# Moving a chunked attention's later units by a few pieces inside a stream of dense matmuls

## The chip, the cores and the metric

The kernel runs on one core of a Trainium2 chip. The metric is the device time of one execution in microseconds (us), the median over the runs shown. The engines are named as the profile names them: PE (TensorE matmul), PEld (its weight loads), DVE (VectorE), ACT (ScalarE), POOL (GpSimd) and SP (SyncE, whose queue issues nearly all transfers, "SPq").

## The reference

Two parts stand one behind the other. First a causal linear attention with decay, for 4 batches, 8 heads, 768 positions and a head width of 64:

```
state = gamma[None, :, None, None] * state + np.einsum('bhd,bhe->bhde', k[:, :, t], v[:, :, t])
y[:, :, t] = scale * np.einsum('bhd,bhde->bhe', q[:, :, t], state)
```

Then y is laid out as 3072 tokens of 512 features and goes through a feed-forward block with 2048 hidden features:

```
h = x @ w_in
g = np.maximum(h, 0.0) + np.log1p(np.exp(-np.abs(h)))
return g @ w_out
```

Everything is float32 in and out. The weights arrive as 64-bit floats and are converted in the kernel.

## The kernel before, in words

**Attention units.** The attention is cut into 48 units: 4 batches, 6 chunks of 128 positions each, and 2 halves of 4 heads; unit n has chunk c = (n // 2) % 6. Units 0 to 11 (n below WHOLE) are computed in plain float32. Units 12 to 47, the "later units", split each operand into a high and a low part so that TensorE can take them in its faster one-pass form. A later unit goes through these parts:

- `load_unit`/`load_ahead`: 8 small transfers each for k and q in blocks (tiles kb and qb, or kbys and qbys from a ring of three; line 151), and one each for k and v by tokens (line 178), all issued from SP's queue.
- `decay`: POOL multiplies q (line 205) and v (206) by decay factors.
- `operands`: DVE transposes the blocks (234), ACT and DVE write the high and low parts into kq (238, 239, 241, 242, 243) and vhl (246, 247).
- `scores_first`, `scores_second`: two pairs of matmuls into a PSUM tile sc (273), each summed by a DVE reduction (274); after the second POOL masks (251), ACT rounds to ah (287) and POOL makes the rest al (288).
- `new_state`: matmuls into stp (303).
- `stack_and_outputs`: 20 small matmuls into the PSUM tile yp (351; 12 for the first chunk of a batch), two ACT copies out of it (374), the split into xh (ACT, 375) and xl (DVE, 376); then the state's split (323, 325).

For the later units sc and yp share a single PSUM bank (`attention_bank`, tag "a", one buffer). So the first scores of unit n+1 cannot start until both copies of line 374 have emptied unit n's yp, and the second scores not until the reduction of line 274 has read the first.

**The feed-forward steps.** Four units make a pair of 256 tokens. In a step s, `hidden(s)` multiplies by w_in (lines 423 to 425, three matmuls make one "piece"), `softplus` works on the result (DVE 431, ACT 432, DVE 436, ACT 438 to gh, POOL 440 to gl), and `second(s-2)` multiplies the step before the last by w_out (456 to 458, again three matmuls to a piece). From step 12 on ("paced" steps) a step is 4 hidden pieces and then 4 second pieces, slots 0 to 7. gh has two buffers, so the gh of a step is written once the second pieces of the same step have read the older one.

**What sets the order.** A counter of ticks says when each part of each unit is issued: `PARTS` gives the tick of each part relative to 16 n, since a unit comes every 16 ticks. In the paced steps one tick falls to one piece, and the PE order there is the written one; a turn of 8 steps covers 64 ticks. The other engines, and PE before step 12, are ordered by the scheduler of the tile framework, which may put an instruction ahead of its place in the program. `ticks_for(p)` says up to which tick the work must be issued before the turn of pair p+1 begins; this fixes to which slot a tick falls. Before, outputs (tick 20) fall behind the first second piece of a step, slot 4, and the next unit's first scores (tick 7 of the next 16) behind slot 7, three pieces later.

**Weights.** `convert_weights(f)` turns the 64-bit numbers of one of 16 slices into high and low parts (85 to 98) on ACT, DVE and POOL; `convert_to(n)` issues conversions up to slice n. In steps 4 to 11 a step uses two slices.

Of the kernel before, what the change touches and what calls it, by code (L numbers as in the profile page):

```python
# [19 lines left out]
TWO = 2 * C  # L20
PLACES = 3
WIDE = 512
AHEAD = 2
EARLY = 2
WHOLE = 12
THIRD = 19
TURN = 4
# [6 lines left out]
def decay_attention_then_softplus_ffn(ctx: ExitStack, tc: tile.TileContext, q, k, v, w_in, w_out, qtab, vtab, gtab, out):  # L34
# [74 lines left out]
    def place_of(p):  # L109
        return p if p < PLACES else (1, 0, 2)[p % PLACES]  # L110
# [100 lines left out]
    def attention_bank(n, shape, name):  # L211
        taken.append(n)
        if n < WHOLE and len(taken) % 2:
            return ps_o.tile(shape, F32, name=name, tag="acc3")
        return ps_a.tile(shape, F32, name=name, tag="a")
# [34 lines left out]
    def mask(a):  # L250
        nc.gpsimd.affine_select(a, a, pattern=[[0, HH], [1, C]], compare_op=ALU.is_ge, fill=0.0, base=0, channel_multiplier=-1)  # L251

    def scores_whole(n):
        if n >= WHOLE:
            return
        kq = live[n][0]
        a = attn.tile([P, HH, C], F32, name="a")
        sc = attention_bank(n, [P, HH, C], "sc")
        for h in range(HH):
            nc.tensor.matmul(sc[:, h, :], lhsT=kz[:, h % 2, h // 2, :], rhs=kq[:, h // 2, :], start=True, stop=True)  # L260
        nc.scalar.copy(a, sc)
        mask(a)
        live[n].append(a)
# [3 lines left out]
    def scores_of_pair(n, j):  # L267
        kq = live[n][0]
        if j == 0:
            summed[n] = attn.tile([P, HH, C], F32, name="a")  # L270
        sc = attention_bank(n, [P, 2, 2, C], "sc")
        for par in range(2):
            nc.tensor.matmul(sc[:, par], lhsT=kq[:, 0, par, j, :], rhs=kq[:, 1:, par, j, :], start=True, stop=True)  # L273
        nc.vector.tensor_reduce(summed[n][:, 2 * j:2 * j + 2, :], sc.rearrange("p h t c -> p h c t"), axis=mybir.AxisListType.X, op=ALU.add)  # L274

    def scores_first(n):
        if n >= WHOLE:
            scores_of_pair(n, 0)

    def scores_second(n):  # L280
        if n < WHOLE:
            return
        scores_of_pair(n, 1)
        a = summed.pop(n)
        mask(a)
        ah, al = (attn.tile([P, HH, C], F32R, name=nm) for nm in ("ah", "al"))
        nc.scalar.copy(ah, a)  # L287
        nc.gpsimd.tensor_tensor(al, a, ah.bitcast(F32), op=ALU.subtract)  # L288
        live[n] += [ah, al]
# [90 lines left out]
        stack_state(n)  # L380


    PARTS = {-24: load_unit, -40: load_ahead, -8: decay, 0: operands, 7: scores_first, 8: scores_whole, 10: scores_second, 12: new_state, 20: stack_and_outputs}
    FIRST_TICK = -24
    PERIOD = 16
    TICK = 4
    last_tick = PERIOD * (len(units) - 1) + max(PARTS)

    def tick(n):
        for at, part in PARTS.items():  # L390
            u, r = divmod(n - at, PERIOD)
            if r == 0 and 0 <= u < len(units):
                part(u)
# [12 lines left out]
    def begins(s, p):  # L406
        return s == 0 or p not in steps[s - 1][0]
# [4 lines left out]
    acc, part, hps, sps, gs = {}, {}, {}, {}, {}  # L412
# [31 lines left out]
    def second(s):  # L444
        pairs, fs = steps[s]
        gh, gl = gs.pop(s)
        places = sorted(place_of(p) for p in pairs)
        for p in pairs:
            if begins(s, p):
                odd = p % 2 or p == 0  # L450
                acc[p] = [ps_o.tile([P, DM], F32, name=f"acc{t}", tag=f"acc{t}") for t in ((0, 1) if odd else (2, 3))]
        for k, p, t in ((k, p, t) for k in range(len(fs)) for p in pairs for t in range(2)):
            at = places.index(place_of(p)) * TWO + t * P
            first, last = begins(s, p) and k == 0, ends(s, p) and k == len(fs) - 1
            wt, ts, to = wout[fs[k]], slice(at, at + P), acc[p][t]
            nc.tensor.matmul(to, lhsT=gh[:, k, ts], rhs=wt[:, 0], start=first, stop=False)  # L456
            nc.tensor.matmul(to, lhsT=gh[:, k, ts], rhs=wt[:, 1], start=False, stop=False)  # L457
            nc.tensor.matmul(to, lhsT=gl[:, k, ts], rhs=wt[:, 0], start=False, stop=last)  # L458
            if last:
                write_out(p, t, s < TURN)  # L460
            yield
# [13 lines left out]
        nc.sync.dma_start(out[row:row + P, :], o)  # L475

    def ticks_for(p):
        return min(PERIOD * 4 * (p + 1) + max(PARTS) - PERIOD + TICK + TICK * AHEAD, last_tick + TICK)

    done, loaded, converted = FIRST_TICK, 0, 0  # L480

    def convert_to(n):
        nonlocal loaded, converted
        while converted < min(NF, n):
            convert_weights(converted)
            converted += 1
            if loaded < NF:
                load_weights(loaded)
                loaded += 1
# [105 lines left out]
    for s, (pairs, fs) in enumerate(steps[:ordered]):  # L595
        if s == TURN:
            block_decays()
        convert_to(fs[-1] + 1)
        stages(s)
        convert_to(2 * max(fs[-1] // 2 + 1, s + 1 if s < TURN else TURN + (s - TURN) // 2) + EARLY)  # L600

    with tc.manual_schedule(engines={mybir.EngineType.PE}):
        for s in range(ordered, len(steps) + LAG):
# [31 lines left out]
```

## Time and profile before

| what | value |
|---|---|
| time, median of 3 runs | 701.84 us (701.45 to 701.94) |
| the profiled execution's own time | 701.68 us |
| its span | 700.0 us |
| PE busy | 662.1 us (95%) |
| DVE, ACT, POOL busy | 60%, 52%, 44% of the span |
| granted PE clock, mean over the span | 0.988 |

The time of the profiled execution is 1.68 us more than its span: the span counts from the first instruction recorded to the last. A row of the timeline gives the start in us from the span's start, the duration, the engine, line, operation and tiles, and in brackets the idle time of that engine just before it and what ended it. A row of the waits gives the total idle time, the number of waits and the longest. A row of the windows gives, for a stretch, the busy time of PE, PEld, DVE, ACT and POOL, then the granted clock, the share of the transfers' engines and GB/s.

### The profile page before, as it was taken

What the parts mean: (1) busy time and instruction counts of PE and PEld (TensorE: products, weight loads), DVE (VectorE), ACT (ScalarE), POOL (GpSimd) and SP (SyncE); (2) the same over time, 40 slices, a digit from 0 to 9 for tenths busy, and PEclk for the clock granted to TensorE, in tenths of its full rate; (3) what the DMA queues carried; (4) which work ended last, traced back from release to release, by engine and by line L of the source; (5) the groups of instructions that cost most, each with busy time, mean ns of one, the idle gap of its engine ahead of it and who ended that gap; (6) DMA issues with size and microseconds to landing.
All of it is one profiled execution on the core that took longest, in us unless ns stands there. A gap on an engine that the chain in (4) does not pass through costs nothing.

```text
span 700.0 us, 11837 instructions
## 1 busy us (share of the span) xinstructions
PE 662.1 (95%) x3762; PEld 556.8 (80%) x3762; DVE 417.4 (60%) x756; ACT 361.1 (52%) x799; POOL 310.1 (44%) x330
## 2 busy tenths in 40 slices
PE   7899998789899989999999989999999999999997
PEld 6789997668778777888888778878878888888896
DVE  4778898655568566565756656566567655432221
ACT  5888875534546455555545545465465545422221
POOL 4887766433344533453443434444534533232221
PEclk9999999899999999999999999999999999999999
DMA  9897662121132231132131223122212200000000
GB/s 243 229 281 204 174 171 49 30 67 33 30 75 47 47 76 29 22 78 39 35 79 34 36 41 72 20 39 70 44 33 67 40 8 30 1 1 31 0 31 30
DMA packets 153822, 46.69 MB, mean 67 GB/s; under 512 B 140448, under 2 KB 148640, under 8 KB 153760
## 3 DMA queue, kind: packets, MB, share of 16 engines
q1 hardware_dynamic: 153312, 45.93, 27.6%
q8 instruction: 29, 0.48, 0.3%
q14 instruction: 33, 0.27, 0.1%
q10 hardware_dynamic: 448, 0.01, 0.0%
HBM read 39.60 MB, written 6.29 MB: 66 GB/s over the span
## 4 chain that ended last, share of the span: by engine, by line
PE 52%; ACT 12%; SPq 8%; DVE 8%; DMA 7%; issue 4%; ACTq 0%; POOL 0%; DVEq 0%; POOLq 0%
PE hp L423 9%; PE hp L425 9%; PE hp L424 9%; SPq L151 7%; PE acc L456 7%; PE acc L457 7%; PE acc L458 7%; ACT kq L242 3%; DVE sp L431 3%; ACT kq L241 3%; PE sc L273 3%; DMA kb<-in_k_dram 2%; DMA qb<-in_q_dram 2%; PE stp L303 2%; PE yp L351 2%
## 5 line engine op out<-in xcount | busy, mean ns | idle before, releaser
L440 POOL TENSOR_TENSOR gl<-sp,gh 128x512 fp32r<-128x512 f32 x96 | 124.0, 1292 | 265.4 <-ACT gh L438 263.1
L423 PE MATMUL hp<-xh,winhl 128*128 128x512 f32 (+1 forms) x448 | 163.0, 364 | 1.3 <-ACT winhl L97 0.8
L424 PE MATMUL hp<-xl,winhl 128*128 128x512 f32 (+1 forms) x448 | 162.9, 364 | 0.0
L425 PE MATMUL hp<-xh,winhl 128*128 128x512 f32 (+1 forms) x448 | 162.0, 362 | 0.2 <-POOL winhl L98 0.2
L456 PE MATMUL acc<-wouthl,gh 128*128 128x512 f32 x384 | 156.1, 407 | 2.0 <-ACT gh L438 2.0
L457 PE MATMUL acc<-wouthl,gh 128*128 128x512 f32 x384 | 151.3, 394 | 0.0
L458 PE MATMUL acc<-wouthl,gl 128*128 128x512 f32 x384 | 150.6, 394 | 0.0
L432 ACT ACTIVATE sp<-sp 128x512 f32<-128x512 f32 x96 | 60.4, 630 | 138.6 <-DVE sp L431 138.5
L431 DVE TENSOR_SCALAR sp<-hp 128x512 uint32<-128x512 uint32 x96 | 65.7, 685 | 105.1 <-PE hp L425 103.2
L425 PEld LDWEIGHTS hp<-xh,winhl 128*128 128x128 f32 x448 | 85.2, 190 | 14.1 <-POOL winhl L98 0.6
L423 PEld LDWEIGHTS hp<-xh,winhl 128*128 128x128 f32 x448 | 85.1, 190 | 12.6 <-ACT winhl L97 1.0
L424 PEld LDWEIGHTS hp<-xl,winhl 128*128 128x128 f32 x448 | 85.2, 190 | 10.5
L438 ACT CAST gh<-sp 128x512 fp32r<-128x512 f32 x96 | 59.5, 619 | 57.7 <-PE acc L457 30.0
L456 PEld LDWEIGHTS acc<-wouthl,gh 128*128 128x128 f32 x384 | 73.0, 190 | 15.3 <-ACT gh L438 2.4
L458 PEld LDWEIGHTS acc<-wouthl,gl 128*128 128x128 f32 x384 | 72.3, 189 | 15.6
L457 PEld LDWEIGHTS acc<-wouthl,gh 128*128 128x128 f32 x384 | 73.1, 190 | 12.8
L436 DVE SCALAR_TENSOR_TENSOR sp<-hp,sp 128x512 f32<-128x512 f32 x96 | 64.9, 677 | 26.4 <-ACT sp L432 25.6
L251 POOL TENSOR_SCALAR_AFFINE_SELECT a<-a 128x512 f32<-128x512 f32 x48 | 35.8, 747 | 53.3 <-DVE a L274 47.6
L274 DVE TENSOR_REDUCE a<-sc 128x256 f32<-128x512 f32 x72 | 49.4, 687 | 15.3 <-PE sc L273 14.3
L273 PEld LDWEIGHTS sc<-kq 128*128 128x128 f32 x144 | 25.2, 191 | 34.6 <-ACT kbys L374 11.4
L288 POOL TENSOR_TENSOR al<-a,ah 128x512 fp32r<-128x512 f32 x36 | 47.7, 1325 | 11.3 <-ACT ah L287 9.6
L273 PE MATMUL sc<-kq 128*128 128x256 f32 x144 | 32.3, 307 | 18.5 <-ACT kbys L374 7.0
(94 smaller groups left out, 908.3 us busy)
## 6 DMA issues: line engine op xcount, KB each, us to landing
win<-in_moe_w_in_dram SPq DMA_DIRECT2D x16, 512.0 KB, 4.8
wout<-in_moe_w_out_dram SPq DMA_DIRECT2D x16, 512.0 KB, 4.6
vn<-in_v_dram SPq DMA_DIRECT2D x48, 128.0 KB, 2.8
out_dram<-o SPq DMA_DIRECT2D x24, 256.0 KB, 2.2
vn<-in_k_dram SPq DMA_DIRECT2D x30, 128.0 KB, 2.3
kb<-in_k_dram SPq DMA_DIRECT2D x208, 16.0 KB, 1.7
qb<-in_q_dram SPq DMA_DIRECT2D x208, 16.0 KB, 1.7
qn<-in_q_dram SPq DMA_DIRECT2D x12, 128.0 KB, 4.7
```

What stands on the lines that cost most here:

```text
L273: nc.tensor.matmul(sc[:, par], lhsT=kq[:, 0, par, j, :], rhs=kq[:, 1:, par, j, :], start=True, stop=True)
L423: nc.tensor.matmul(to, lhsT=wt[:, 0, d, :], rhs=xh[:, d], start=d == 0, stop=False)
L424: nc.tensor.matmul(to, lhsT=wt[:, 0, d, :], rhs=xl[:, d], start=False, stop=False)
L425: nc.tensor.matmul(to, lhsT=wt[:, 1, d, :], rhs=xh[:, d], start=False, stop=d == ND - 1)
L431: nc.vector.tensor_scalar(sp.bitcast(U32), hps[s].bitcast(U32), 0x80000000, None, op0=ALU.bitwise_or)
L432: nc.scalar.activation(sp, sp, AF.Softplus)
L436: nc.vector.scalar_tensor_tensor(g, hps.pop(s), 0.0, g, op0=ALU.max, op1=ALU.add)
L438: nc.scalar.copy(gh, g)
L440: nc.gpsimd.tensor_tensor(gl, sps.pop(s), gh.bitcast(F32), op=ALU.subtract)
L456: nc.tensor.matmul(to, lhsT=gh[:, k, ts], rhs=wt[:, 0], start=first, stop=False)
L457: nc.tensor.matmul(to, lhsT=gh[:, k, ts], rhs=wt[:, 1], start=False, stop=False)
L458: nc.tensor.matmul(to, lhsT=gl[:, k, ts], rhs=wt[:, 0], start=False, stop=last)
```

## The change

Four things are edited:

1. For the later units (`of_others`) the parts move: loads from tick -24 to -20, the two scores from 7 and 10 to 14 and 17, the state from 12 to 18, outputs from 20 to 26. Operands stay at 0 and decay at -8. The table for units 0 to 11 (`of_whole`) is as before.
2. `ticks_for` gives 16 ticks beyond 64 (p + 1) for pairs 0 and 1, as before, and 19 for later pairs (16 before). So outputs now fall behind slot 7, the end of a step, the first scores behind slot 3, four hidden pieces later, and the second scores behind slot 6.
3. In the one step in which both pairs of a turn begin, `second` takes the pairs in reversed order.
4. `convert_to` at the end of steps 4 to 8 asks for slices 12, 13, 14, 15 and 16, where it asked for 10, 10, 12, 12 and 14.

```
-AHEAD = 2
+AHEAD = 9
...
-    PARTS = {-24: load_unit, -40: load_ahead, -8: decay, 0: operands, 7: scores_first, 8: scores_whole, 10: scores_second, 12: new_state, 20: stack_and_outputs}
+
+    def of_whole(part):
+        return lambda n: part(n) if n < WHOLE else None
+
+    def of_others(part):
+        return lambda n: part(n) if n >= WHOLE else None
+
+    PARTS = {-24: of_whole(load_unit), -20: of_others(load_unit), -40: load_ahead, -8: decay, 0: operands}
+    PARTS.update({8: of_whole(scores_whole), 12: of_whole(new_state), 20: of_whole(stack_and_outputs)})
+    PARTS.update({14: of_others(scores_first), 17: of_others(scores_second), 18: of_others(new_state), 26: of_others(stack_and_outputs)})
...
+        if len(pairs) > 1 and all(begins(s, p) for p in pairs):
+            pairs = pairs[::-1]
...
-        return min(PERIOD * 4 * (p + 1) + max(PARTS) - PERIOD + TICK + TICK * AHEAD, last_tick + TICK)
+        return min(PERIOD * 4 * (p + 1) + (PERIOD if p < 2 else max(PARTS) - PERIOD + AHEAD), last_tick + TICK)
...
-        convert_to(2 * max(fs[-1] // 2 + 1, s + 1 if s < TURN else TURN + (s - TURN) // 2) + EARLY)
+        convert_to((2 * (s + 1) if s < TURN else TURN + s + 2) + EARLY)
```

The rows of the changed kernel below carry its own line numbers (423 to 425 are 427 to 429 there, 456 to 458 are 462 to 464, 351 is 346, 273 is 271, 303 is 298, 432 is 436, 438 is 442, 440 is 444, 374 is 369, 375 is 370, 323 is 318, 287 is 282, 288 is 283; lines up to 251 keep theirs).

**PE, a later unit in the paced steps.** Before, from the outputs (yp) to the next unit's first scores (sc):

```order
L351 MATMUL yp<-al,vhl 64x128 x4
L456 MATMUL acc_4697<-wouthl,gh 128x512
...
L456 MATMUL acc_5270<-wouthl,gh 128x512
...
L456 MATMUL acc_5271<-wouthl,gh 128x512
L457 MATMUL acc_5271<-wouthl,gh 128x512
L458 MATMUL acc_5271<-wouthl,gl 128x512
L273 MATMUL sc<-kq_84 128x256 x2
L423 MATMUL hp<-xh,winhl 128x512
```

and now:

```order
L464 MATMUL acc_5271<-wouthl,gl 128x512
L346 MATMUL yp<-kq_84,st_5172 64x128 x2
...
L346 MATMUL yp<-al,vhl 64x128 x4
L427 MATMUL hp<-xh,winhl 128x512
L428 MATMUL hp<-xl,winhl 128x512
L429 MATMUL hp<-xh,winhl 128x512
...
L271 MATMUL sc<-kq_85 128x256 x2
L462 MATMUL acc_4696<-wouthl,gh 128x512
```

Three second pieces stood between; now it is the four hidden pieces of the next step, with the scores in front of its second pieces.

**ACT at the same place.** sp and gh are the softplus, 241, 242 and 238 the operands of the unit after next, st the state, the copies qbys<-yp empty the bank. Before:

```order
L432 ACTIVATE sp<-sp 128x512
L241 CAST kq_85<-qb 64x256
L242 CAST kq_85<-qb 64x256
L241 CAST kq_85<-qb 64x256
L323 CAST st_4426<-stp 64x128 x2
L242 CAST kq_85<-qb 64x256
L374 COPY qbys<-yp 64x256 x2
L246 CAST vhl<-vn_90 128x4x64
L438 CAST gh<-sp 128x512
L375 CAST xh<-qbys 128x2x128
```

and now:

```order
L442 CAST gh<-sp 128x512
L241 CAST kq_85<-qb 64x256
L242 CAST kq_85<-qb 64x256
L241 CAST kq_85<-qb 64x256
L318 CAST st_4453<-stp 64x128 x2
L242 CAST kq_85<-qb 64x256
L369 COPY qbys<-yp 64x256 x2
L246 CAST vhl<-vn_90 128x4x64
L370 CAST xh<-qbys 128x2x128
L436 ACTIVATE sp<-sp 128x512
```

The run of operand writes, state and copies is the same; gh moved from behind the copies to ahead of the operand writes, and the next step's softplus stands behind all of it.

**PE where the paced steps begin (about 115 us).** hp of 128x256 is step 11, the last before the paced steps, hp of 128x512 is step 12; the last half of step 11 needs the slice of w_in that is converted last. Before:

```order
L303 MATMUL stp<-vn_90 128x128 x2
L423 MATMUL hp<-xh,winhl 128x512
...
L273 MATMUL sc<-kq_84 128x256 x2
...
L423 MATMUL hp<-xh,winhl 128x256
...
L456 MATMUL acc_1038<-wouthl,gh 128x512
...
L425 MATMUL hp<-xh,winhl 128x256
...
L273 MATMUL sc<-kq_84 128x256 x2
L351 MATMUL yp<-ah,vhl 64x128 x8
```

and now:

```order
L429 MATMUL hp<-xh,winhl 128x512
L271 MATMUL sc<-kq_84 128x256 x2
L427 MATMUL hp<-xh,winhl 128x256
L428 MATMUL hp<-xl,winhl 128x256
L429 MATMUL hp<-xh,winhl 128x256
...
L271 MATMUL sc<-kq_84 128x256 x2
L298 MATMUL stp<-vn_90 128x128 x2
L427 MATMUL hp<-xh,winhl 128x512
...
L346 MATMUL yp<-ah,vhl 64x128 x8
```

One piece of step 12 stands ahead of the last half of step 11, where four stood; the other three, and four second pieces of step 10, now stand between the second scores and yp. On ACT, DVE and POOL everything up to here is in the order of before, the weight conversions among it, except that ACT writes the very last slice of w_out ahead of the state st.

**POOL in the paced steps.** gl belongs to the softplus, qb to the decay of a unit further on, a to the mask. Before:

```order
L440 TENSOR_TENSOR gl<-sp,gh 128x512
L251 AFFINE_SELECT a<-a 128x512
L205 TENSOR_TENSOR qbys<-qbys,qblocks 128x256
L288 TENSOR_TENSOR al<-a,ah 128x512
L440 TENSOR_TENSOR gl<-sp,gh 128x512
```

and now:

```order
L444 TENSOR_TENSOR gl<-sp,gh 128x512
L205 TENSOR_TENSOR qb<-qb,qblocks 128x256
L251 AFFINE_SELECT a<-a 128x512
L444 TENSOR_TENSOR gl<-sp,gh 128x512
L283 TENSOR_TENSOR al<-a,ah 128x512
```

The decay of q moved ahead of the mask, and one gl ahead of al.

More of the change, by code (lines that the diff above doesn't have):

```diff
@@ L253, in scores_whole @@
     def scores_whole(n):
-        if n >= WHOLE:
-            return
         kq = live[n][0]
@@ L276, in scores_first @@
     def scores_first(n):
-        if n >= WHOLE:
-            scores_of_pair(n, 0)
+        scores_of_pair(n, 0)
     def scores_second(n):
-        if n < WHOLE:
-            return
         scores_of_pair(n, 1)
```

## Prediction

> **What bounds the kernel now.** I read the busy table first, then PE's waits, the windows for the granted clock, and the timeline of single units.
>
> ```profile
> PE 662.1 (95%) x3762; PEld 556.8 (80%) x3762; DVE 417.4 (60%) x756; ACT 361.1 (52%) x799; POOL 310.1 (44%) x330
> ```
>
> PE is the bound: nothing is gained by making another engine faster, only by taking PE's idle and slow time away. The work of PE itself does not change. Its waits after the first 100 us, those that matter here:
>
> ```profile
> PE sc L273 <- ACT kbys L374: 7.0, 10, 1.9
> PE sc L273 <- ACT qbys L374: 5.9, 11, 1.1
> PE yp L351 <- ACT ah L287: 4.6, 1, 4.6
> PE sc L273 <- ACT vn L374: 4.1, 4, 2.5
> PE acc L456 <- ACT gh L438: 2.0, 1, 2.0
> PE sc L273 <- DVE a L274: 1.4, 2, 0.8
> PE hp L423 <- ACT winhl L97: 0.8, 1, 0.8
> ```
>
> 25 of them, 17.0 us in all, are one thing: the first scores of a later unit wait for the copies (374) that empty the bank of the previous unit's yp. And PE runs at half clock for a while after the longer ones:
>
> ```profile
> 125.00:150.00 25.00, 21.59 (x100) 17.37 (x100) 15.38 (x26) 11.04 (x26) 10.28 (x10) 0.83 0.23 52
> 175.00:200.00 25.00, 21.70 (x110) 17.66 (x109) 15.90 (x29) 12.55 (x31) 8.56 (x10) 0.93 0.18 34
> 400.00:450.00 50.00, 47.09 (x251) 38.63 (x252) 29.89 (x55) 25.00 (x58) 21.37 (x23) 0.97 0.22 46
> ...
> 142.29 0.47 PE L456 MATMUL acc<-wouthl,gh 128*128 128x512 f32 x1 [1.97 <-ACT gh L438]
> ...
> 144.45 0.63 PE L457 MATMUL acc<-wouthl,gh 128*128 128x512 f32 x1
> ```
>
> Clocks of 0.83, 0.93 and 0.97 are (0.17 x 25) + (0.07 x 25) + (0.03 x 50) = 7.5 us lost; about 0.8 of it falls into idle time, so 6.7 us count, behind four waits (4.6, 2.0 and the longest two for line 374), 1.7 each. The last two rows show it: behind an idle 1.97 us a matmul of 512 columns lasts 0.63 us instead of the usual 0.4.
>
> **The main edit: outputs at a step's end, scores four pieces later.** A usual unit before, PE first and then ACT:
>
> ```profile
> 507.12 0.28 PE L351 MATMUL yp<-kq,st 128*64 128x128 f32 x2
> ...
> 508.32 0.45 PE L456 MATMUL acc<-wouthl,gh 128*128 128x512 f32 x1
> ...
> 511.02 0.50 PE L273 MATMUL sc<-kq 128*128 128x256 f32 x2 [0.40 <-ACT qbys L374]
> ...
> 510.22 0.74 ACT L374 COPY qbys<-yp 64x256 f32<-64x256 f32 x2
> ```
>
> ACT empties the bank at 510.96, 3.84 us after yp began, because the operand writes and the state stand ahead of the copies in its order. PE has 1.20 us of yp and three pieces to do meanwhile. One unit near the end of the attention already stands as the change puts all of them, since the last turn's ticks slide against the pieces (PE, ACT, DVE):
>
> ```profile
> 592.35 0.28 PE L351 MATMUL yp<-kq,st 128*64 128x128 f32 x2
> ...
> 593.54 0.45 PE L423 MATMUL hp<-xh,winhl 128*128 128x512 f32 x1
> ...
> 596.36 0.40 PE L273 MATMUL sc<-kq 128*128 128x256 f32 x2
> ...
> 598.69 0.50 PE L273 MATMUL sc<-kq 128*128 128x256 f32 x2
> ...
> 595.35 0.74 ACT L374 COPY qbys<-yp 64x256 f32<-64x256 f32 x2
> ...
> 596.90 0.42 DVE L376 TENSOR_TENSOR xl<-qbys,xh 128x256 fp32r<-128x256 f32 x1
> ```
>
> There four hidden pieces take 596.36 - 593.54 = 2.82 us, 0.705 each, the bank is empty at 596.09, 3.74 us after yp began, and the scores follow at 4.01 us without a wait. The slack is 0.27 us, and nothing in the changed ACT order stands ahead of the copies that did not stand there in this unit. So the 25 waits go. Each costs more than its idle time: by three pieces of 0.705 from 508.32 the scores were due at 510.44 and came at 511.02, 0.58 us later, of which 0.40 idle; the other 0.18 is refilling PE. Saved: 17.0 + 25 x 0.18 = **21.5 us**. The two DVE waits (1.4 + 0.4) go too, **1.8**; one of them returns as a rival below.
>
> What takes their place: the second scores need the reduction (274) of the first, three pieces after them. In unit 592.35 they start at 598.69, where 596.36 + 0.23 + 3 x 0.69 = 598.66 was due, and their own row is 0.50 instead of 0.40 long: 0.13 us in all. I charge this for all 33 later units that have a successor in such a place: **4.3 us**. The bounds are 0 and the 0.65 + 0.18 of the unit in the next fence, 27.4; the value is taken near the low end, from the row in the same order.
>
> Loads at tick -20 instead of -24 come four pieces, 2.8 us, later in the program. All 16 block transfers and the two by tokens of a unit move with them, in SP's queue. I cost it at nothing, because those transfers wait for a free buffer and not for their place:
>
> ```profile
> SPq L151 <- DVE kq L243: 79.3, 27, 4.4
> SPq L151 <- DVE kq L239: 50.6, 32, 6.2
> ...
> 395.67 0.28 PE L351 MATMUL yp<-kq,st 128*64 128x128 f32 x2
> ...
> 395.58 0.45 DVE L234 STREAM_TRANSPOSE kb<-kb 128x256 f32<-128x256 f32 x1 [3.44 <-DMA kb<-in_k_dram]
> ...
> 398.52 3.83 SPq L151 DMA_DIRECT2D qb<-in_q_dram  x8
> ...
> qb<-in_q_dram SPq DMA_DIRECT2D x208, 16.0 KB, 1.7
> ```
>
> The 395.58 row is a late transfer that holds DVE; before, the transpose stood ahead of the step's softplus (431), which delayed sp, the operand writes and the copies, hence the longer waits of the list. In the changed order it stands behind the softplus, so up to about 2 us of lateness ends in DVE's idle time. If that cover goes, the third rival below has the price.
>
> **Where the paced steps begin.** Here yp of the first later unit waited 4.6 us for ah right behind its scores. Now three hidden and four second pieces (7 x 0.69 = 4.8 us) and stp stand between, and saved are 4.6 + 0.18 = **4.8 us**. The wait of 2.0 for gh at 142.29 was the last link of the same congestion (+0.18: **2.2**). The half clock behind all these waits is the **6.7** worked out above. But one stall is new:
>
> ```profile
> 115.59 0.48 PE L423 MATMUL hp<-xh,winhl 128*128 128x512 f32 x1
> ...
> 116.92 0.62 ACT L97 CAST winhl<-w 128x512 fp32r<-128x512 f32 x1 [2.75 <-DVE w L95]
> ...
> 117.62 1.30 POOL L98 TENSOR_TENSOR winhl<-w,winhl 128x512 fp32r<-128x512 f32 x1 [1.19 <-ACT winhl L97]
> ...
> 126.13 1.11 PE L351 MATMUL yp<-ah,vhl 128*64 128x128 f32 x8 [4.63 <-ACT ah L287]
> ```
>
> The last half of step 11 needs the high part of its weights (117.54) and then the low part (118.92). Before, step 12 filled PE until then. Now one piece (0.7) and the scores (0.25) fill it from about 115.23, without stp, to 116.2: PE idles 1.3 us, runs two matmuls, and idles 1.1 us more. With 2 x 0.18 of refill that is 2.8, and 2.4 us idle within 3 us should halve the clock as 1.97 did; the clock's share of one such wait is 1.7. Charged: **4.5 us**; bounds 0 (the weights come earlier) and, should the half clock last twice as long, 6.2.
>
> [...]
>
> **Weights a step sooner: nothing.** Up to the high part of the last w_in slice the four engines keep the order of before; the scheduler had already put conversions where their inputs allow. So the 0.8 us wait for winhl stays, and I count no gain. The reversed pairs of one step start on the accumulators that are not just being emptied:
>
> ```profile
> 141.47 0.68 DVE L473 COPY o<-acc 128x512 f32<-128x512 f32 x1
> ```
>
> This copy ends at 142.15, as gh does, so the reversal helps to take away the 2.2 already counted and brings nothing of its own.
>
> **The sum.** 21.5 + 1.8 + 4.8 + 2.2 + 6.7 = 37.0 removed, 4.3 + 4.5 = 8.8 added: 28.2 less. The profiled span of 700.0 becomes 671.8, and with the 1.68 us between span and time **673.5 us** (the profiled execution, 701.68, stands 0.16 below the median).
>
> **The rivals.**
>
> *The second scores become the new wait.* The unit before the one above, PE, DVE and POOL:
>
> ```profile
> 584.03 0.51 PE L273 MATMUL sc<-kq 128*128 128x256 f32 x2 [0.65 <-DVE a L274]
> ...
> 581.95 1.31 DVE L376 TENSOR_TENSOR xl<-kbys,xh 128x256 fp32r<-128x256 f32 x1 [0.40 <-ACT xh L375]
> ...
> 581.69 1.29 POOL L440 TENSOR_TENSOR gl<-sp,gh 128x512 fp32r<-128x512 f32 x1 [6.42 <-ACT gh L438]
> ```
>
> Here xl on DVE stretched from 0.42 to 1.31 us beside gl on POOL; the reduction behind it came late, and PE idled 0.65. If that happens in every unit, 33 x 0.83 = 27.4 replaces 4.3: 673.5 + 23.1 = 696.6. Against it: gh, and so gl, now starts as yp does and is over 2 us later, when xl, at about 4.5 us, is still to come. For it: other POOL work could fall there. [...]
>
> *The transfers of the two-buffer units stay late.* In units 13 to 19 the loads have only two buffers. If three of them still stall as before at 178 us (2.5 idle, 0.2 refill, 1.5 of half clock: 4.2 each), it is 673.5 + 12.6 = 686. For it: SP's queue waits 130 us for DVE; against it: the two us of cover above.
>
> *The weights do come sooner.* Then the new stall of 4.5 and the old 0.8 + 0.18 vanish: 668. Against it is the unchanged order.
>
> The rows of POOL for the last rival:
>
> ```profile
> L205 POOL TENSOR_TENSOR qb<-qb,qblocks 128x256 f32<-128x256 f32 x26 | 16.5, 636 | 9.2 <-DMA qb<-in_q_dram 7.0 <-DMA kb<-in_k_dram 1.6 <-DMA vn<-in_v_dram 0.4
> L251 POOL TENSOR_SCALAR_AFFINE_SELECT a<-a 128x512 f32<-128x512 f32 x48 | 35.8, 747 | 53.3 <-DVE a L274 47.6
> L288 POOL TENSOR_TENSOR al<-a,ah 128x512 fp32r<-128x512 f32 x36 | 47.7, 1325 | 11.3 <-ACT ah L287 9.6
> ```
>
> *Slower: POOL's decay holds the mask.* qb (205) now stands ahead of the mask (251). In the unit of 395.67 its eight transfers are issued by 402.35 and the last lands 1.7 later, 8.4 us after yp began. POOL's qb (0.64), mask (0.75), gl (1.29) and al (1.33) follow, so al is ready near 12.4 us; the next yp begins after about 13 (16 pieces of 0.69, yp, the scores, stp) and needs al 1.0 later: 1.6 us of slack. It decides once qb lands more than 1.6 us later. Should the four-tick delay come through in full, 2.8 us, each unit loses 1.2 + 0.18, and 33 of them 46: 673.5 + 46 = 719. Against it: the transfers are bound by buffers, not by ticks.
>
> **How the numbers follow.** Forecast (673.5, its own range 667 to 680): 0.65. Late transfers (686): 0.13. Second scores (697): 0.11. Weights sooner (668): 0.06. Slower (719): 0.05. The range 666 to 692 leaves out the slower case, the upper part of the second scores, and a little below: under 0.2. All cases but the last are faster by more than 0.2%, 1.4 us, which is about what a measurement of this kernel can tell from no change; some of the second-scores case might end there, so faster 0.92, same 0.03, slower 0.05.
>
> **What would show it.** Right: the waits of sc for line 374 all but gone; PE's idle total from 150 to 600 us down to a few us; a granted clock of 1.00 in the windows from 150 us on; one stall of about 2.4 us near 117 us for winhl, and yp of the first later unit without a wait. Wrong: sc waiting for the reduction in most units with xl stretched (second scores), DVE held by kb or qb with PE idle behind it (transfers), or yp waiting for al (slower).

## The result, and the profile after

The changed kernel takes 673.77 us (672.65 to 674.67 in 4 runs), beside 701.64 us (700.34 to 701.94) of the kernel before on the same chip: a ratio of 0.9605, with a 95% interval of 0.9586 to 0.9624. The forecast was 673.5. The profiled execution took 673.9 us, with a span of 672.1.

The busy times of the changed kernel, from the head of its page, and PE's waits behind the start (total idle us, number, longest):

```profile
PE 654.8 (97%) x3762; PEld 553.8 (82%) x3762; DVE 414.9 (62%) x756; ACT 367.8 (55%) x799; POOL 311.6 (46%) x330
...
PE sc L271 <- DVE a L272: 3.2, 3, 1.2
PE hp L427 <- ACT winhl L97: 1.5, 2, 0.8
PE hp L429 <- POOL winhl L98: 1.0, 2, 0.8
PE sc L271 <- ACT kbys L369: 0.7, 2, 0.4
PE sc L271 <- ACT vn L369: 0.3, 1, 0.3
PE sc L271 <- DVE xl L338: 0.3, 1, 0.3
```

The first scores waited 17.0 us for ACT's copies; now it is 1.0. The 4.6 us of the first later unit's outputs and the 2.0 us for gh are gone from the list. The stall for converted weights is new, and the second scores' waits for the reduction (272) grew from 1.4 to 3.2 us.

The windows of the changed kernel (length, busy us of PE, PEld, DVE, ACT, POOL, then the granted clock, share of the transfers' engines, GB/s):

```profile
100.00:125.00 25.00, 22.18 (x120) 18.78 (x119) 21.72 (x38) 14.41 (x31) 15.62 (x16) 0.93 0.27 51
125.00:150.00 25.00, 25.00 (x136) 21.02 (x135) 18.49 (x31) 13.99 (x31) 14.00 (x14) 1.00 0.28 63
175.00:200.00 25.00, 25.00 (x143) 20.59 (x142) 16.10 (x32) 13.40 (x31) 11.95 (x13) 1.00 0.31 66
400.00:450.00 50.00, 49.70 (x281) 41.38 (x281) 31.35 (x58) 28.13 (x64) 23.91 (x24) 1.00 0.24 48
```

Where the clock was 0.83, 0.93 and 0.97, it is 1.00. One slow stretch is left, from 117.4 to 120.8 us, at these two rows of the timeline; the second already runs at half clock:

```profile
116.42 0.39 PE L427 MATMUL hp<-xh,winhl 128*128 128x256 f32 x1 [0.74 <-ACT winhl L97]
...
117.77 0.58 PE L429 MATMUL hp<-xh,winhl 128*128 128x256 f32 x1 [0.85 <-POOL winhl L98]
```

A steady unit, from its outputs to the next unit's (PE, then ACT's copies in a unit of the same kind):

```profile
312.74 0.28 PE L346 MATMUL yp<-kq,st 128*64 128x128 f32 x2
...
316.76 0.40 PE L271 MATMUL sc<-kq 128*128 128x256 f32 x2
319.09 0.50 PE L271 MATMUL sc<-kq 128*128 128x256 f32 x2
326.04 0.28 PE L346 MATMUL yp<-kq,st 128*64 128x128 f32 x2
...
383.11 0.74 ACT L369 COPY qbys<-yp 64x256 f32<-64x256 f32 x2
```

The copies end 383.85 - 380.10 = 3.75 us after that unit's yp (380.10), and the scores come 4.02 us after theirs, without a wait. The unit takes 13.30 us. The three waits for the reduction (at 159, 214 and 373 us, 0.8 to 1.2 us each) come from late transfers. The last of them, DVE first and then PE:

```profile
369.16 0.45 DVE L234 STREAM_TRANSPOSE kb<-kb 128x256 f32<-128x256 f32 x1 [3.69 <-DMA kb<-in_k_dram]
...
371.81 0.69 DVE L435 TENSOR_SCALAR sp<-hp 128x512 uint32<-128x512 uint32 x1
372.42 0.68 DVE L272 TENSOR_REDUCE a<-sc 128x256 f32<-128x512 f32 x1
...
373.15 0.50 PE L271 MATMUL sc<-kq 128*128 128x256 f32 x2 [0.78 <-DVE a L272]
```

A late kb held DVE 3.69 us, everything behind it slid without a gap, and the reduction came after the second scores were due.

### The profile page after: what moved, and what is told of

Read it like the earlier page. It is cut to its first block, busy times and chain, and to the rows that moved or that the text cites. A ratio compares the mean times of both kernels' runs of the same rounds, so it can differ in the third digit from the quotient of the medians.

```text
span 672.1 us, 11849 instructions
## 1 busy us (share of the span) xinstructions
PE 654.8 (97%) x3762; PEld 553.8 (82%) x3762; DVE 414.9 (62%) x756; ACT 367.8 (55%) x799; POOL 311.6 (46%) x330
## 4 chain that ended last, share of the span: by engine, by line
PE 73%; DVE 9%; ACT 6%; DMA 5%; SPq 3%; issue 2%; POOL 1%; DVEq 0%; POOLq 0%; ACTq 0%
PE acc L462 10%; PE acc L463 10%; PE acc L464 10%; PE hp L427 10%; PE hp L429 10%; PE hp L428 10%; PE yp L346 5%; SPq L151 3%; PE sc L271 3%; DMA kb<-in_k_dram 3%; PE stp L298 2%; DVE kq L239 2%; DVE sp L435 1%; PE sc L258 1%; DVE kq L243 1%
## 5 line engine op out<-in xcount | busy, mean ns | idle before, releaser
L444 POOL TENSOR_TENSOR gl<-sp,gh 128x512 fp32r<-128x512 f32 x96 | 128.1, 1335 | 130.0 <-ACT gh L442 125.7
L427 PE MATMUL hp<-xh,winhl 128*128 128x512 f32 (+1 forms) x448 | 166.6, 372 | 2.1 <-ACT winhl L97 1.5
L429 PE MATMUL hp<-xh,winhl 128*128 128x512 f32 (+1 forms) x448 | 162.6, 363 | 1.0 <-POOL winhl L98 1.0
L462 PE MATMUL acc<-wouthl,gh 128*128 128x512 f32 x384 | 150.9, 393 | 0.0
L463 PE MATMUL acc<-wouthl,gh 128*128 128x512 f32 x384 | 150.2, 391 | 0.0
L464 PE MATMUL acc<-wouthl,gl 128*128 128x512 f32 x384 | 149.0, 390 | 0.0
L462 PEld LDWEIGHTS acc<-wouthl,gh 128*128 128x128 f32 x384 | 72.2, 188 | 12.3
L463 PEld LDWEIGHTS acc<-wouthl,gh 128*128 128x128 f32 x384 | 72.3, 188 | 12.0
L205 POOL TENSOR_TENSOR qb<-qb,qblocks 128x256 f32<-128x256 f32 x26 | 17.2, 663 | 87.1 <-ACT gh L442 27.0
L206 POOL TENSOR_TENSOR vn<-vn,vtabs 128x256 f32<-128x256 f32 x48 | 30.7, 639 | 38.5 <-DMA vn<-in_v_dram 25.7
L251 POOL TENSOR_SCALAR_AFFINE_SELECT a<-a 128x512 f32<-128x512 f32 x48 | 33.5, 699 | 21.2 <-DVE a L272 14.5
```

The lines of the kernel that those rows point to most:

```text
L427: nc.tensor.matmul(to, lhsT=wt[:, 0, d, :], rhs=xh[:, d], start=d == 0, stop=False)
L429: nc.tensor.matmul(to, lhsT=wt[:, 1, d, :], rhs=xh[:, d], start=False, stop=d == ND - 1)
L444: nc.gpsimd.tensor_tensor(gl, sps.pop(s), gh.bitcast(F32), op=ALU.subtract)
```

## The experiments

Diffs marked "after" are against the changed kernel, those marked "before" against the kernel before. Times are medians of four runs (two where both are given), and each ratio is to runs of the kernel before on the same chip. The runs were made on several chips, so two of them are also compared by their ratios, where a difference of 0.001 stands for 0.7 us.

### Is it the distance or the place?

The prediction took the outputs' new place and the added piece as one edit. Three kernels part them, though none has the new place alone at three pieces: the first of them keeps the reversed pairs, the later loads and the earlier conversion of the change.

*One piece less, place as changed (after):*

```
-PARTS.update({14: of_others(scores_first), 17: of_others(scores_second), ...
+PARTS.update({13: of_others(scores_first), 16: of_others(scores_second), ...
```

> The changed kernel with one piece less between the operands and each pair's scores: first scores of the later units at tick 13, second at 16; outputs stay at the step's end. Theory (the distance is what paid): in the changed kernel the first scores come 4.01 us after the unit's operands and the ScalarE copies end 3.75 us after them; one piece (0.66 us) earlier they are due at 3.35 and wait about 0.4 us, and with 0.18 us of refill that is 0.58 us in each of about 25 units, some 15 us: about 689 us, with 8 to 11 us of idle time of the first scores put down to ScalarE. Rival (what paid is that the outputs lie at the step's end, away from the scores): no such wait comes back, 674 us.

*One piece more, place as before (before):*

```
-PARTS = {..., 7: scores_first, 8: scores_whole, 10: scores_second, ...
+PARTS = {..., 8: scores_first_and_whole, 11: scores_second, ...
```

> The kernel before with its scores one piece later and nothing else: first scores at tick 8, second at 11, outputs and the rest at the old places in the middle of a step. Theory: the usual short waits of the first scores for ScalarE (about 20 at 0.5 to 0.6 us, with 0.18 us of refill some 14 us) go, and the four long ones with the half clock behind them, 4.6 us of wait of the first later unit's outputs and 2.2 us of an accumulator's wait stay: 685 to 690 us. Rival (the distance alone gives the whole gain): 674 us. Second rival (position alone): about 700 us.

*The change with the old place (after; `ticks_for` gives 16 for all pairs):*

```
-PARTS.update({14: of_others(scores_first), 17: of_others(scores_second), 18: of_others(new_state), 26: of_others(stack_and_outputs)})
+PARTS.update({8: scores_first_and_whole, 11: of_others(scores_second), 12: new_state, 20: stack_and_outputs})
```

> The changed kernel with the outputs and all else of the later units moved back six ticks (scores at 8 and 11, state 12, outputs 20, as in the middle of a step), so that it has the added piece, the loads at -20, the reversed pairs and the earlier conversion, and not the outputs at the step's end. From the run that changed only the scores' distance (674.7 us, one wait of 4.6 us of the first later unit's outputs, one of 1.5 us of an accumulator's first matmul, a half clock of some 3 us behind them) the theory says: the 4.6 us wait comes back, and the accumulator's is taken away by the reversed pairs: 672 to 675 us, with a steady unit of 13.18 us in place of 13.29. Rival (the outputs' place pays or costs in every unit): outside 670 to 677 us.

| | outputs in the middle of a step | outputs at its end |
|---|---|---|
| three pieces to the scores | before: 703.7 and 700.0 us beside these runs | 682.27 us, ratio 0.9697 (0.9671 to 0.9723) |
| four pieces | 674.67 us, ratio 0.9593 (0.9563 to 0.9624); with the other edits 673.3 us, 0.9614 (0.9592 to 0.9637) | the change: ratio 0.9605 |

The added piece alone gives the whole gain, with the loads at -24 as before. The outputs' place, together with the three small edits, gives some 20 us at three pieces and nothing at four: the two take away losses that overlap. At three pieces 8.8 of the 17.0 us of first-score waits stay, but the half clock (1.00 from 100 us on), the 4.6 and the 2.0 us are gone. With the added piece alone the first-score waits are gone, and the 4.6 us stay with 6.8 us of half clock around them (clock 0.97 and 0.89 over 100 to 125 and 125 to 150 us). My theory for that run (685 to 690 us) fell because it kept the long waits of the first scores and the half clock behind them, and those went too; the rival that the distance alone gives the whole gain was right. What the theory had right were the two waits that stay. The waits of that run, and the row of the run with one piece less in which the usual wait comes back:

```profile
PE yp L355 <- ACT ah L291: 4.6, 1, 4.6
PE sc L273 <- DVE a L274: 2.3, 2, 1.4
PE acc L460 <- DVE o L477: 1.5, 1, 1.5
```

```profile
318.39 0.50 PE L271 MATMUL sc<-kq 128*128 128x256 f32 x2 [0.31 <-ACT kbys L369]
```

That wait, 24 of them, sums to 8.8 us, inside the 8 to 11 expected. The time rose by only 8.5 us (6.5 by the ratios) instead of 15. A steady unit takes 13.73 us: 0.57 us more than the 13.16 of a unit without wait or edge (below), as expected, but only 0.43 more than the 13.30 of the changed kernel, whose edge it no longer has. And one wait of 0.9 us for the reduction is left of three with 3.2.

With four pieces the place still moves two things, in opposite ways. At the first later unit the old place waits 4.6 us. In the steady units behind it is faster. The run of the change with the old place, PE and then DVE in a steady unit:

```profile
339.62 0.28 PE L346 MATMUL yp<-kq,st 128*64 128x128 f32 x2
...
352.78 0.28 PE L346 MATMUL yp<-kq,st 128*64 128x128 f32 x2
```

```profile
344.27 0.41 DVE L371 TENSOR_TENSOR xl<-kbys,xh 128x256 fp32r<-128x256 f32 x1
344.71 0.69 DVE L272 TENSOR_REDUCE a<-sc 128x256 f32<-128x512 f32 x1
346.21 0.69 DVE L437 TENSOR_SCALAR sp<-hp 128x512 uint32<-128x512 uint32 x1 [0.80 <-PE sc L271]
```

The unit takes 13.16 us in place of 13.30. The first reduction stands ahead of the step's softplus, with 0.80 us of idle time on DVE behind it. In the changed kernel the softplus (435, at 371.81 above) stands between xl and the reduction, and DVE has no gap there. That is the second scores' edge, and with no gap there a late kb still reaches PE at 214 and 373 us. The run with the old place has two such waits, at 148 and 163 us and 3.1 us in all, and none later. PE's work, counted by the columns of its matmuls, shows what both sides come to: at the work that the old place has done by 167.0 us the change is 6.9 us ahead (160.1), and at the end of the span it is 0.9 us behind (672.1 beside 671.2).

### The second scores one piece later (after)

```
-PARTS.update({14: ..., 17: of_others(scores_second), 18: of_others(new_state), 26: ...})
+PARTS.update({14: ..., 18: of_others(scores_second_and_state), 26: ...})
```

> The changed kernel with only the second scores of the later units one piece later, in front of the state's work of the same unit at tick 18. Theory: the edge of 0.13 us at each of 33 second scores (4.3 us) and the three waits of 1.2 us for VectorE's reduction go; the masks come one piece later, with room to spare ahead of the outputs at tick 26: 666 to 670 us. Rival (the second scores' edge is no wait but the time of the matmul itself, and only the three waits go): 670 to 671 us. Rival on the other side (the later mask and state delay the outputs): above 674 us.

It took 689.8 us, ratio 0.9806 (0.9775 to 0.9837): 16 us slower than the change (14 by the ratios). The side "above 674" holds, by a way that none of the theories named. DVE, POOL, ACT and PE of one unit:

```profile
395.36 0.50 PE L271 MATMUL sc<-kq 128*128 128x256 f32 x2
...
399.52 0.62 POOL L205 TENSOR_TENSOR qb<-qb,qblocks 128x256 f32<-128x256 f32 x1 [8.86 <-DMA vn<-in_v_dram]
...
400.17 0.45 DVE L234 STREAM_TRANSPOSE qb<-qb 128x256 f32<-128x256 f32 x1 [4.07 <-DMA vn<-in_k_dram]
400.54 0.65 DVE L272 TENSOR_REDUCE a<-sc 128x256 f32<-128x512 f32 x1
...
402.86 0.33 PE L346 MATMUL yp<-ah,vhl 128*64 128x128 f32 x2 [0.95 <-ACT ah L282]
```

The second scores were written by 395.9, but their reduction ran at 400.54: the scheduler now put it behind the transpose of a later unit's qb, which waited for POOL's decay, and that for transfers. (POOL's row ends at 400.14; the transfer that the profile names beside the transpose fills another tile.) The mask, ah and yp followed late, and with them the buffers for the next transfers. This is no single case: in 22 of the 36 later units the second reduction starts 1.4 to 4.7 us after its scores, in the changed kernel never more than 1.2. There the reduction stands ahead of that transpose:

```profile
387.10 0.68 DVE L272 TENSOR_REDUCE a<-sc 128x256 f32<-128x512 f32 x1
...
388.92 0.45 DVE L234 STREAM_TRANSPOSE qb<-qb 128x256 f32<-128x256 f32 x1 [0.69 <-POOL qb L205]
```

One piece decides on which side it falls.

### The stall where the paced steps begin (after)

```
-return min(PERIOD * 4 * (p + 1) + (PERIOD if p < 2 else max(PARTS) - PERIOD + AHEAD), last_tick + TICK)
+return min(PERIOD * 4 * (p + 1) + (PERIOD if p < 3 else max(PARTS) - PERIOD + AHEAD), last_tick + TICK)
```

> The changed kernel with one more pair of slices paced by the short rule at the start of the paced steps (one constant of the tick count), which moves hidden pieces there. Theory: the stall for the converted weights at 109 to 118 us (2.4 us idle, and the half clock at 117.4 to 120.8 us for 1.7 us) shrinks, at most by 4.5 us: 669 to 674 us. Rival: the work only moves and the wait for the weights comes elsewhere in the same region: 673 to 676 us.

It took 672.88 us (0.9563, 0.9533 to 0.9594). The waits for weights stayed (0.78, 0.18, 0.61 and 0.85 us at 112 to 120 us), and PE waited 0.83 us for softplus at 127 us; the half clock did not come (mean clock 1.000). The waits only moved, as the rival has it, but the time fits the theory's 669 to 674: 0.9 us below the change, 2.9 us by the ratios, whose intervals just overlap. What the trace shows as gained is the half clock, absent (mean clock 1.000) in three of the four executions here and in one of four of the changed kernel, and where that falls is partly chance (last section). So this run does not decide.

The slice itself, left out (slice 15 of w_in is not loaded nor converted, and slice 14 stands in its place):

```
+            if bits is None:
+                to[f] = to[f - 1]
+                continue
             words = bits.bitcast(U32)
```

> The changed kernel in which the last slice of the first layer's weights is neither loaded nor converted; slice 14 stands in for it (that part of the result is another). Theory: the stall for that slice's converted weights at 116 to 118 us is real work that nothing else covers: 0.90 and 1.01 us of idle time and the half clock at 117.4 to 120.8 us (1.7 us) go, 3.6 us: 670.2 us. Rival (the engines there are full and the next converted weights or a unit's operands stall at once): 672 to 674 us.

It took 670.85 us (0.9582, 0.9540 to 0.9624), which by the time alone fits the theory (670.2), though by the ratios the gain over the change is 1.6 us, with overlapping intervals. The trace tells another story:

```profile
117.93 0.50 PE L278 MATMUL sc<-kq 128*128 128x256 f32 x2 [1.88 <-DVE a L279]
...
116.58 0.69 DVE L447 SCALAR_TENSOR_TENSOR sp<-hp,sp 128x512 f32<-128x512 f32 x1 [0.76 <-ACT sp L443]
117.19 0.68 DVE L279 TENSOR_REDUCE a<-sc 128x256 f32<-128x512 f32 x1
```

The waits for the weights are gone, and at the same place PE waits 1.88 us for a reduction behind the softplus, with one stretch of half clock behind it (0.93 over 100 to 125 us). Summed from the starts of the matmuls, some 1.4 of the expected 3.6 us were gained at 100 to 125 us; most of the rest of the trace's gain lies at 148 to 160 us, where the changed kernel has its first wait for a late transfer and this run has none. So the rival is right for the place: the weights are only the first thing to be late there, and behind them comes the softplus, whose DVE part waits for ACT's in turn. DVE is busy for 6.97 of the 8.00 us from 110 to 118 us.

*The pairs in the old sequence (after):*

```
-        if len(pairs) > 1 and all(begins(s, p) for p in pairs):
-            pairs = pairs[::-1]
```

> The changed kernel without the reversal of the two pairs in the step that begins both. Theory of the prediction (reversal alone gives nothing): 673.8 us, within 1 us. Rival (the reversal is what removed the wait of 1.5 to 2.2 us of an accumulator's first matmul at 142 us): 675.5 to 677.5 us, with that wait back, and perhaps a half clock of 1.7 us behind it.

673.76 us (0.9612, 0.9588 to 0.9635): the reversal gives nothing of its own, and no accumulator waits.

### The loads, and the time of conversion (after)

```
-    PARTS = {-24: of_whole(load_unit), -20: of_others(load_unit), -40: load_ahead, -8: decay, 0: operands}
+    PARTS = {-24: load_unit, -40: load_ahead, -8: decay, 0: operands}
```

> The changed kernel with the loads of all units at -24 in place of -20 for the later ones. Theory (a buffer's release sets the start of those loads, so that their place in the order is worth nothing): 673.8 us, within 1 us, and the three waits of 1.2 us of second scores for VectorE's reduction stay. Rival (the later place of the loads caused the late transfers of three units): 669 to 671 us without these waits.

With outputs at 26, loads at -24 stand ahead (two ticks) of the outputs of the unit three before, which in units below 19 pass through the tile of values that these loads fill; so in those units another value results, from work of the same size. It took 676.68 us (0.9648, 0.9622 to 0.9674), and neither theory held: the three waits for the reduction are gone, and a single longer one came, with half clock behind it (0.63 us for the next matmuls of 512 columns, usually 0.39).

```profile
201.46 0.60 PE L271 MATMUL sc<-kq 128*128 128x256 f32 x2 [3.34 <-ACT vn L369]
```

As the order of writing and reading a tile differs, this run cannot say what four ticks alone are worth; it shows that -20 goes with outputs at 26.

```
-        convert_to((2 * (s + 1) if s < TURN else TURN + s + 2) + EARLY)
+        convert_to(2 * max(fs[-1] // 2 + 1, s + 1 if s < TURN else TURN + (s - TURN) // 2) + EARLY)
```

> The changed kernel with the old rule for when weights are converted. The order of instructions is the same on every engine as the changed kernel's, so both theories expect its time, 673.8 us; a difference of over 1 us would mean that the place of buffers or the spread of such runs is larger than the terms judged here.

675.01 us (673.18 to 676.50; 0.9647, 0.9608 to 0.9687), 1.2 us above the change, with the same order on every engine and overlapping intervals. Differences of 1 us between two kernels are therefore not told by times here, only by the waits in their traces.

### A version that takes both sides (after)

The first two later units keep outputs at 26; from the third on the parts stand at 8, 11, 12 and 20, and `ticks_for` gives 16 for all pairs:

```
+    for at, part in ((-20, load_unit), (14, scores_first), (17, scores_second), (18, new_state), (26, stack_and_outputs)):
+        place(at, part, WHOLE, WHOLE + 2)
+    for at, part in ((-20, load_unit), (8, scores_first), (11, scores_second), (12, new_state), (20, stack_and_outputs)):
+        place(at, part, WHOLE + 2, len(units))
```

> The changed kernel in which only the first two later units have their outputs at the step's end; from the third on the four parts lie six ticks earlier, at 8, 11, 12 and 20, with the same four pieces to the first scores. Theory (the outputs' place pays once, at the first later unit, and costs from then on: three waits of 1.2 us for late transfers and 0.11 us at each of some 31 second scores): the changed kernel's time less 3.6 and 3.4 us, some 665 to 668 us. Rival (what the first units save, the third waits for): 672 to 675 us.

669.21 us (667.49 to 670.31), ratio 0.9548 (0.9524 to 0.9573): its interval lies below that of the change, and it beats both kernels. PE is busy throughout, where the changed kernel had 49.70:

```profile
400.00:450.00 50.00, 50.00 (x278) 41.96 (x277) 31.76 (x64) 29.15 (x69) 21.97 (x23) 1.00 0.22 45
```

It lies a little above the 665 to 668 expected; waits of 0.6 to 1.0 us remain at 117, 118, 125, 156, 549 and 563 us. An attempt on the first three:

```
-        return min(PERIOD * 4 * (p + 1) + PERIOD, last_tick + TICK)
+        return min(PERIOD * 4 * (p + 1) + PERIOD - (8 if p == 2 else 0), last_tick + TICK)
```

> The kernel of 669.2 us with the attention work of the first paced steps' start eight ticks later (one constant of the tick count), so that the weights' conversion has VectorE and ScalarE more to itself at 100 to 125 us. Theory: its waits for converted weights and for softplus there (0.4, 0.3, 0.8, 1.0 and 1.0 us) shrink: 666 to 669 us. Rival (the first later units then come too late, and wait at their scores): 670 to 674 us.

672.73 us (0.9616, 0.9581 to 0.9650): the rival. What the start saves, the second later unit gives back, with a stretch of half clock behind this row (0.63 us for matmuls of 512 columns from 148.75 us on):

```profile
146.42 0.66 PE L346 MATMUL yp<-ah,vhl 128*64 128x128 f32 x8 [2.83 <-ACT gh L462]
```

### The price of a wait (on the version of 669.2 us)

```
-        for par, own, oth in sides:
-            nc.scalar.copy(ys[own], yp[:, par])
+        for _ in range(1 + MORE.get(n, 0)):
+            for par, own, oth in sides:
+                nc.scalar.copy(ys[own], yp[:, par])
```

> The kernel of 669.2 us (outputs of only the first two later units at the step's end) with waits of known size put in: in nine units, 13 us or more apart, ScalarE's two copies of yp, which free the bank of the first scores, are made 2 to 6 times more often (units 17, 20, 26, 28, 30, 32, 38, 40, 42: 3, 4, 2, 3, 4, 5, 3, 4, 6 pairs more, of 0.74 us each; the same values are written again). The copies ended 0.18 us before the scores, so the waits should be 1.3, 2.1, 2.8, 3.5 and 4.3 us for 2, 3, 4, 5 and 6 pairs, 24 us in all, and 1.6 us of refill. Theory from the traces so far (a window of 3.41 us on a fixed grid in which TensorE idles over 2.07 us halves the clock of the next window): about five of the nine halve it, those with over 2.07 us of their idle time inside one window, and none with less, at 1.7 us each: some 703 us, and the records of the clock must agree window by window. Rival (each wait of 2 us or more halves it, as the prediction priced it): eight, 708 us. [...]

It took 719.51 us (two runs, 719.11 and 719.92), above both numbers. The waits were longer than meant, as the scheduler let vhl and gh slip between the copies. With their refill the nine were 2.6, 3.8, 2.3, 3.1, 3.8, 4.6, 3.1, 3.8 and 5.4 us, 32.5 in all. So the sums decide nothing, but each wait can be read by itself. Two of them are equal; PE, and then windows of 3.41 us, laid so that one begins where the trace's clock falls to 0.50, at 354.91 us:

```profile
354.93 0.80 PE L272 MATMUL sc<-kq 128*128 128x256 f32 x2 [2.89 <-ACT kbys L371]
503.44 0.50 PE L272 MATMUL sc<-kq 128*128 128x256 f32 x2 [2.88 <-ACT kbys L371]
```

```profile
351.50:354.91 3.41, 0.54 (x3) 0.11 (x1) 0.43 (x1) 3.23 (x10) 1.26 (x1) 1.00 0.23 36
354.91:358.32 3.41, 3.40 (x9) 2.82 (x10) 1.47 (x3) 0.40 (x1) 0.61 (x1) 0.50 0.03 7
498.33:501.74 3.41, 2.23 (x10) 1.50 (x8) 2.34 (x7) 3.23 (x10) 0.00 (x0) 1.00 0.09 15
501.74:505.15 3.41, 1.71 (x8) 1.47 (x9) 1.12 (x2) 1.98 (x6) 1.76 (x2) 1.00 0.15 24
505.15:508.57 3.42, 3.42 (x19) 2.94 (x18) 2.90 (x5) 1.69 (x4) 0.93 (x2) 1.00 0.01 2
```

The wait of 2.89 us lay in one window, in which PE was idle for 2.87 us, and the next ran at 0.50. The wait of 2.88 us was split over two, idle for 1.18 and 1.70 us, and the next ran at 1.00. Seven of the nine were followed by a window at 0.50; the run's mean clock is 0.969. The two that were not are the one above and the one of 2.3 us, split over two windows that idle 0.83 and 1.28 us. The rival "2 us or more" fails on both of them. In the five windows at 1.00 named here the theory's 2.07 us lies between what was enough (2.87) and what was not (1.70 and less); the figure itself is an estimate that this run does not narrow.

## Why the prediction was right

**The size.** Forecast span 671.8, measured 672.1; net 28.2 us expected, 27.9 found. So close a hit is luck: four executions of the changed kernel differ by 2 us (670.8 to 672.8), and errors in the terms cancel. By terms:

- *25 waits of the first scores, 21.5 us.* Right: 17.0 us of idle time became 1.0, by the mechanism named. The scores come at 4.02 us and the bank is empty at 3.75 (forecast 4.01 and 3.74).
- *The two waits for DVE, 1.8.* Right, the units that had them wait no more; three others came, see the last term.
- *The waits of the first later unit (4.8) and of the accumulator (2.2).* Right, both are gone. They come back (4.6 and 1.5 us) in the run with the old place and no reversal, and the first alone in the run with the old place and the reversal. Since the run at the new place without the reversal has neither, either of the two edits is enough for the accumulator.
- *The half clock, 6.7.* Right in sum: the three slow windows are at 1.00. Its price per wait was a mean that no single wait has (below). And one of the four waits was misread: behind the second longest wait for line 374 (1.87 us) the clock stayed whole, and the stretch of half clock at 416.7 us lies behind a shorter one (1.78 us). These are the rows of the kernel before:

```profile
250.43 0.51 PE L273 MATMUL sc<-kq 128*128 128x256 f32 x2 [1.87 <-ACT kbys L374]
...
415.49 0.50 PE L273 MATMUL sc<-kq 128*128 128x256 f32 x2 [1.78 <-ACT kbys L374]
```

- *The second scores' edge, 0.13 us for 33 units, 4.3.* Right in size for a unit: 13.30 against 13.16 us where it is absent. But only 17 units show it, with second scores 2.32 to 2.34 us after the first; others have 2.30, as in the run without the edge, or another wait instead. That is 2.2 us.
- *The new stall at 117 us, 4.5.* Right in place and kind; measured idle 0.74 and 0.85 us where 1.3 and 1.1 were expected, and one stretch of 3.41 us at half clock, as charged. From the scores at 115.17 to the end of that stretch at 120.82 us PE lost 3.6 us, compared with its pace at 111 us (0.12 us for a matmul of 256 columns). That the half clock came is in part luck: in the run without the reversal, with the same two waits (0.74 and 0.85 us), the mean clock was 1.000.
- *Not charged: three waits for late transfers, 3.6 us with refill.* The step "up to about 2 us of lateness ends in DVE's idle time" failed: behind a late kb DVE has no idle time until the reduction. It was the rival of the late transfers, come in three units at 0.8 to 1.2 us each instead of 4.2 each.

So two terms were charged 3.0 us too high together, and one of 3.6 us was missing, as were the 1.0 us that the first scores still wait. The terms as corrected give 26 to 27 of the 27.9 us; the runs' spread does not let me place the rest.

**The attribution.** The prediction's heading gave the 21.5 us to "outputs at a step's end, scores four pieces later" together. The runs show that the second half of this does it. Moving the outputs took away the 4.6 us, with the half clock around it, and brought the stall at 117 us: 6.9 us ahead of the old place at 160 us, where the old place has its own two waits for the reduction behind it as well. From there on it lost 7.8 us: the edge (2.2), the two late transfers at 214 and 373 us (2.2), and smaller waits that I did not break down. Nothing net. The prediction had the first waits, the edge and the stall as numbers and never set them against each other.

**The other rivals.** Second scores: xl stays at 0.42 us, and the wait appears in three units only. Weights sooner: no, the 0.8 us wait at 109 us stayed, and so did the order. Slower through POOL's decay: not in the change, but real one piece further. In the run with later second scores the decay, late by its transfers, held the reduction by way of DVE and not the mask on POOL, and cost 14 to 16 us.

## What to carry to other kernels

When an edit changes a distance and a place at once, price them apart: two ways to take away the same wait do not add. Read the slack on the engine behind the one that waits (here DVE between xl and the reduction), since it decides whether a late transfer reaches the bound. And before moving one more piece, see which instruction of the next unit it passes: the gain goes by tenths of a microsecond and the loss by the whole wait of what it lands behind.

## What the runs showed of the hardware

Up to the last matmul, the trace of the kernel before has four stretches at a clock of 0.50: from 123.12 us for 6.83 us, and from 143.60, 177.73 and 416.67 us for 3.41 us each. Their starts lie 20.48, 34.13 and 238.93 us apart, 6, 10 and 70 times 3.413. The changed kernel has one, from 117.41 us for 3.41 us.

I cut both traces into windows of 3.413 us from these starts, and counted as idle the time from one matmul's start to the next beyond the median for its line and width (0.227 us for 512 columns, 0.12 for 256, 0.06 for the 128 of yp in a later unit). The windows at full clock right ahead of a stretch at 0.50 idled 2.09, 2.20, 2.27 and 2.07 us in the kernel before (from 119.7, 140.2, 174.3 and 413.3 us) and 2.20 us in the changed one (from 114.0 us). From 60 us to the last matmul all other windows at full clock idled 1.51 us or less. Earlier one idled 2.08 us, from 18.4 us in the changed kernel, and the clock stayed at 1.00 behind it; so these traces give no limit. The two rows of the kernel before differ in the same way: the wait of 1.78 us lies within the window from 413.3 to 416.7 us, the one of 1.87 us is cut at 249.4 us, into windows that idled 1.11 and 1.15 us.

Behind a window at 0.50 less was enough in the run with the longer copies. The second of these three windows was idle for 1.29 us and another at 0.50 followed it, while behind the window at 1.00 that was idle for 1.70 us (from 501.74 us) none came:

```profile
529.00:532.41 3.41, 1.04 (x5) 0.53 (x3) 0.64 (x2) 3.26 (x9) 0.90 (x1) 1.00 0.22 36
532.41:535.82 3.41, 2.12 (x6) 1.84 (x7) 1.47 (x3) 1.56 (x5) 0.97 (x2) 0.50 0.03 5
535.82:539.23 3.41, 3.41 (x10) 2.73 (x10) 0.86 (x2) 0.63 (x2) 0.00 (x0) 0.50 0.02 5
```

Short waits came to the same as a long one: at 117 us none was above 0.85 us. And of the two waits of 2.9 us above, one was followed by 3.41 us at half clock, which is 1.7 us of work, and one by none. Where the stretches fall differs between executions of one kernel: of four of the changed kernel three show a mean clock of 0.996 or 0.997, and one 1.000, with the shortest span (670.8 us).

A matmul in plain float32 (line 260 of the kernel before, 48 of them with 128 columns) left two records each in the trace, with 0.11 us from start to start, and one on high and low parts (line 273, 144 of them with 256 columns) a single record, with 0.12 us.
